# Attention and Fourier-mix kernel: q, k and v loads in half tiles on a new timetable, converted weights stored slot by slot

## The chip, the cores and the metric

The kernel runs on one core of a Trainium2 chip. The metric is the device time of one execution in microseconds (us), lower is better. All times are of undisturbed ("fast") runs.

## The reference, cut to what matters

```python
# q, k, v: (8, 12, 448, 64); x is the attention output as (8, 448, 768)
scores = einsum('bhij,hg->bgij', q @ k^T / 8, w_pre)     # heads mixed before the softmax
attn   = softmax(scores); attn = einsum('bhij,hg->bgij', attn, w_post)   # and after
x      = attn @ v
u      = x + real(fft(fft(x, axis=seq), axis=d_model))
out    = u + relu(layernorm(u) @ w_ch1) @ w_ch2          # w_ch1, w_ch2 arrive as float64
```

## The kernel before

There are two stages. The **mixing stage** does attention and the Fourier mix; the **feed-forward stage** the two large products. The mixing stage is one software pipeline of 192 steps, 24 per batch. In every step TensorE (PE) does a pre-mix product (tile mx), a post-mix product (po), and one or two of QK^T, attention times v (AV) and transposes; VectorE (DVE) a row maximum and a block transpose; ScalarE (ACT) the exponentials and most copies. GpSimd (POOL) has three jobs in one in-order queue: it scales the softmax, it "folds" the rows for the Fourier transform (additions of half and quarter rows), and it issues the DMAs for q, k, v and the weights.

The fold of a batch is dealt from a list. What the step may take of it depends on whether the step also took something from the list of loads:

```python
    while s < TOT or any(fill.values()):
        n = take("none", s)               # loads due in this step (POOL issues them)
        ...                               # premix, postmix, max, exp, AV, transpose
        if s >= 4:
            wts.deal(1)                   # one DVE operation of the weight conversion
        ...                               # QK, gather of step s+4 (SP), scale of step s+2 (POOL)
        for _ in range(min(len(folds), 1 if n and s > 3 else 2)):
            folds.pop(0)()                # one POOL operation (some are three)
        take("full", s)                   # transposes, emit_x, emit_z, emit_s2
        s += 1

    def emit_z(b, par, y):                # Fourier product; needs the whole fold
        while ("xf", par) not in batches[b] or folds:
            folds.pop(0)()
        ...
```

q and k loads are timed from their use, v loads come whole, one pair of heads a step, and a converted weight item (seven tiles) is stored in one DMA:

```python
            old = loads[-4] + 2 if len(loads) > 3 else -99
            for y in range(2):
                due("none", max(old, f + a - GS - 5) + y, lambda ...: emit_load_qk(b, xx, nm, y))
        ...
        for pr in range(3):
            due("none", f + AT_AV[-1][pr] + 2, lambda ...: emit_load_v(b, pr))   # both halves
    ...
        def store():                      # _Weights.add
            nc.gpsimd.dma_start(out=dst.rearrange("k p f -> p k f"), in_=box["st"][:, :, :w])
```

"Local step" means the step within the batch, 0 to 23. The second half of a batch's fold (12 entries) is queued at the end of local step 5 of the *next* batch, and emit_z wants it at the end of local step 14.

## Time and profile before

| | before |
|---|---|
| time, median (range) | 2551.49 us (2550.93 to 2552.16) |
| span of the profiled run | 2549.6 us |
| first block transpose of the pipeline | 43.2 us |
| its 192 steps, first start to last | 900.0 us |
| from the last step's start to the end | 1606.5 us |

The last three rows come from the starts of the DVE block transposes, one per step, in the timeline. Differences between those starts are "step lengths"; a step length holds both a stall and the slow matmuls after it.

The rows of the groups by line for POOL (out<-in, count, busy us and mean ns, then idle before) price what the change moves:

```profile
L569 POOL TENSOR_TENSOR xs<-X 113x384 f32<-113x384 f32 x64 | 64.3, 1019 | 0.3
L374 POOL DMA_DIRECT2D rawk<-in_k_dram x84 | 61.1, 729 | 0.0
L382 POOL DMA_DIRECT2D vv<-in_v_dram x48 | 30.6, 640 | 0.0
L253 POOL DMA_DIRECT2D w<-wst x30 | 28.8, 961 | 117.8 <-DVE wst L250 115.6 <-DVE rcp L475 2.2
```

The reader is to see that issuing a DMA occupies POOL for 0.64 to 0.96 us, about as long as a fold operation (1.02 us). Of q and k 24 DMAs are issued per batch, 17.5 us of POOL time. The 0.0 us of idle time before the k and v issues means that POOL always came to them straight from other work; of these issues only the stores waited.

### The profile page before, as it was taken

The numbers are of one execution on the slowest core, as the hardware profiler recorded it, in microseconds if no ns is written. First come the engines' busy times: TensorE is split into PE (matmuls) and PEld (weight loads), VectorE is DVE, ScalarE is ACT, GpSimd is POOL, SyncE is SP. The second block draws the span as 40 slices with busy tenths as digits, with TensorE's granted clock in tenths as the row PEclk, the third lists the DMA queues.
The fourth block names the chain that finished last, engine by engine and source line by source line (L and its number), as shares of the span: only waits on it lengthen the run. The fifth ranks groups of instructions, "written<-read, shape, count | busy, mean of one in ns | idle before, by whom it ended". The sixth has DMA issues, their size and how long they took to land.

```text
span 2549.6 us, 47913 instructions
## 1 busy us (share of the span) xinstructions
PE 2404.3 (94%) x18608; PEld 1557.3 (61%) x18608; DVE 1513.6 (59%) x3103; ACT 791.8 (31%) x2059; POOL 695.8 (27%) x1112
## 2 busy tenths in 40 slices
PE   6899998979898985999999999999999999999999
PEld 2344443534444444677777777777777777777776
DVE  3666767757677764778456636663666366633333
ACT  3575656646565642232211111111111111011110
POOL 2565758575756652111000000000000000000000
PEclk9899999989899997999999999999999999999999
DMA  4544546363544545544444444444444444343331
GB/s 123 165 152 143 169 134 182 119 170 134 167 153 131 168 140 184 183 152 165 180 145 136 147 155 143 138 147 150 141 146 140 154 136 150 129 155 115 133 112 50
DMA packets 165311, 372.05 MB, mean 146 GB/s; under 512 B 33854, under 2 KB 87126, under 8 KB 165086
## 3 DMA queue, kind: packets, MB, share of 16 engines
q1 hardware_dynamic: 129038, 260.22, 31.0%
q0 software_dynamic: 30480, 107.39, 14.0%
q8 instruction: 149, 2.44, 0.4%
q10 hardware_dynamic: 5568, 1.38, 0.3%
q14 instruction: 76, 0.62, 0.1%
HBM read 211.98 MB, written 74.34 MB: 112 GB/s over the span
## 4 chain that ended last, share of the span: by engine, by line
PE 82%; POOL 5%; ACT 4%; DVE 4%; DMA 3%; issue 2%; SPq 1%; ACTq 0%; POOLq 0%; DVEq 0%
PE psP L896 17%; PE psP L950 17%; PE psR L896 9%; PE psR L950 9%; PE mx L451 6%; PE ms L515 5%; PE psQ L950 4%; PE psQ L896 4%; PE po L488 4%; PE ms L425 3%; ACT PP L467 3%; DMA Kr<-Sb 3%; DVE nmx L459 2%; PE ms L613 1%; PE ms L629 1%
## 5 line engine op out<-in xcount | busy, mean ns | idle before, releaser
L896 PE MATMUL psP<-ub,w1t 128*128 128x256 f32 x2016 | 462.9, 379 | 0.0
L950 PE MATMUL psP<-w2t,h 128*128 128x384 f32 x1344 | 460.9, 486 | 0.0
L896 PEld LDWEIGHTS psP<-ub,w1t 128*128 128x128 f32 x2016 | 382.8, 190 | 60.7
L950 PEld LDWEIGHTS psP<-w2t,h 128*128 128x128 f32 x1344 | 254.4, 190 | 165.9
L478 POOL TENSOR_SCALAR PP<-PP,rcp 128x448 f32<-128x448 f32 x384 | 242.4, 642 | 355.9 <-DVE rcp L476 280.9
L204 POOL DMA_DIRECT2D raw<-in_moe_w_ch_dram x120 | 69.8, 582 | 988.4 <-DVE tmp L242 969.3
L467 ACT ACTIVATE PP<-mx,nmx 128x448 f32<-128x448 f32 x384 | 240.3, 631 | 290.1 <-DVE nmx L459 277.9
L459 DVE TENSOR_REDUCE nmx<-mx 128x1 f32<-128x448 f32 x384 | 221.6, 619 | 148.0 <-PE mx L451 137.7
L956 DVE TENSOR_TENSOR u<-u,psP 128x384 f32<-128x384 f32 x336 | 183.6, 553 | 143.5 <-PE psP L950 141.3
L901 ACT COPY h<-psP 128x512 f32<-128x512 f32 x42 | 24.6, 587 | 761.7 <-PE psP L896 761.7
L451 PE MATMUL mx<-Kr,kw 60*64 60x448 f32 x1536 | 211.4, 566 | 51.8 <-ACT PP L467 39.8
L896 PE MATMUL psR<-ub,w1t 128*128 128x256 f32 x1008 | 231.4, 379 | 0.0
L950 PE MATMUL psR<-w2t,h 128*128 128x384 f32 x672 | 230.5, 486 | 0.0
L499 DVE STREAM_TRANSPOSE Pv<-po 128x896 f32<-128x896 f32 x192 | 212.7, 1108 | 6.7 <-PE po L488 6.7
L896 PEld LDWEIGHTS psR<-ub,w1t 128*128 128x128 f32 x1008 | 191.4, 190 | 26.3 <-DVE ub L875 0.3
L907 DVE TENSOR_TENSOR h<-h,psQ 128x512 f32<-128x512 f32 x42 | 28.9, 688 | 295.5 <-PE psQ L896 295.5
L307 ACT COPY Sb<-ms 124x448 f32<-124x448 f32 x384 | 184.9, 541 | 21.7 <-DMA Kr<-Sb 16.0
L488 PE MATMUL po<-PP,kw 60*32 60x448 f32 x3072 | 191.0, 554 | 0.0
L515 PEld LDWEIGHTS ms<-Pv,vv 64*64 64x64 f32 x5376 | 145.3, 134 | 73.5 <-issue 33.8
L425 PE MATMUL ms<-kT,qT 64*60 64x448 f32 (+1 forms) x1536 | 189.7, 556 | 0.0
L950 PEld LDWEIGHTS psR<-w2t,h 128*128 128x128 f32 x672 | 127.2, 190 | 87.4
L515 PE MATMUL ms<-Pv,vv 64*64 64x120 f32 x5376 | 169.3, 270 | 2.2 <-issue 2.2
(92 smaller groups left out, 2680.8 us busy)
## 6 DMA issues: line engine op xcount, KB each, us to landing
ub<-ub SPq DMA_DIRECT2D x294, 384.0 KB
Kr<-Sb SPq DMA_DIRECT2D x768, 105.0 KB
raw<-in_moe_w_ch_dram POOLq DMA_DIRECT2D x72, 256.0 KB, 3.1
raw<-in_moe_w_ch_dram POOLq DMA_DIRECT2D x48, 384.0 KB, 3.4
w<-wst POOLq DMA_DIRECT2D x18, 896.0 KB, 4.7
w<-wst POOLq DMA_DIRECT2D x12, 1344.0 KB, 5.8
w1t<-w SPq DMA_DIRECT2D x42, 384.0 KB
w2t<-w SPq DMA_DIRECT2D x42, 384.0 KB
```

Source lines behind the costliest of these rows:

```text
L307: (nc.scalar.copy if eng == "a" else nc.vector.tensor_copy)(out=out, in_=in_)
L425: nc.tensor.matmul(pss[x][64 * y:64 * y + r0 + 64 - lo, :S], st["qT", xx][64 * x:64 * x + 64, y, lo:r0 + 64], st["kT", xx][64 * x:64 * x + ...
L451: nc.tensor.matmul(mx[64 * z:64 * z + 64, x, :S], kw1[64 * x:64 * x + KR, :], Kr[64 * x:64 * x + KR, z, :], start=True, stop=True)
L459: nc.vector.tensor_reduce(nmx[:, x:x + 1], steps[T]["mx"][:, x, :S], axis=AX.X, op=ALU.max, negate=True)
L467: nc.scalar.activation(PP[:, x, :], steps[T]["mx"][:, x, :S], ACTF.Exp, bias=steps[T]["nmx"][:, x:x + 1], accum_out=den[:, x:x + 1])
L478: nc.gpsimd.tensor_scalar(PP[:, x, :], PP[:, x, :], rcp[:, x:x + 1], 1.0, op0=ALU.mult, op1=ALU.mult)
L488: nc.tensor.matmul(po[o:o + 32, z, :S], kw2[64 * z:64 * z + KR, y, :], PP[64 * z:64 * z + KR, :, c * HS:(c + 1) * HS], start=True, stop=True)
L499: nc.vector.transpose(g["Pv"][:, T % GT, :].rearrange("p (z s) -> p z s", z=2), steps[T]["po"][:, :, :S])
L515: nc.tensor.matmul(pss[y][64 * x:64 * x + 64, :nu * R], st["v", pr][64 * y:64 * y + 64, x, jb * D:(jb + 1) * D], _ap(Pv, 64 * y * rp + 32 ...
L896: nc.tensor.matmul(p[:, m, :], w1[i][:, kc, m * P:(m + 1) * P], ub[:, kc, :], start=i in OPENS and m == kc == 0, stop=kc == NK - 1, skip_g ...
L950: nc.tensor.matmul(p, lhs[i][:, kf, x * P:(x + 1) * P], w2[i][:, kf, :], start=i in OPENS and kf == 0, stop=kf == FM - 1, skip_group_check ...
L956: nc.vector.tensor_tensor(us_, us_, p, op=ALU.add)
```

## The change

The intent: at most one half tile is loaded a step (only the last two halves of v share one, step 7), and of the steps 6 to 12, in which POOL is to fold the second half, only 8 and 12 have a q or k load; only q and k loads now hold the folding to one operation; a weight item leaves in seven small stores, each a step after the DVE operation that made it.

```diff
+AT_L = ((-4, -3), (-2, -1), (0, 1), (2, 8), (12, 13), (14, 15))   # local steps of the q/k halves
+AT_V = ((3, 4), (5, 6), (7, 7))                                   # and of the v halves
@@ _Weights.add: a tile for each slot, and a store for each slot
+        def new(slot):
+            box[slot] = self.pst.tile([P, DH], F32, name="wst", tag=f"wst{slot}")[:, :w]
+        def store(slot):
+            self.later.append(lambda: nc.gpsimd.dma_start(out=dst[slot], in_=box[slot]))
...
-        self.ops.append((store, False))
@@ deal
+        while self.later:
+            self.later.pop(0)()
         while self.ops and (n > 0 or not self.ops[0][1]):
@@ q/k
-                due("none", max(old, f + a - GS - 5) + y,
+                due("none", f + at[y] - GS,
@@ v
-            due("none", f + AT_AV[-1][pr] + 2, lambda b=b, pr=pr: emit_load_v(b, pr))
+            for y in range(2):
+                due("none", f + AT_V[pr][y], lambda b=b, pr=pr, y=y: emit_load_v(b, pr, y))
@@ take: only q/k loads return True and count
-        n0 = len(fill[kind])
+        large = 0
...
-                fn()
+                large += bool(fn())
...
-        return n0 - len(fill[kind])
+        return large
```

## The prediction

> **What bounds the kernel now.** I read the page first, then stage windows, then the waits, then the timeline around the longest gaps. The slices of the page part the run in two: a talking-heads stage up to about 1000 us, and a feed-forward stage after it.
>
> ```profile
> PE   6899998979898985999999999999999999999999
> POOL 2565758575756652111000000000000000000000
> DMA  4544546363544545544444444444444444343331
> ```
>
> The windows by stage (columns: stretch, length, busy us and count of PE, PEld, DVE, ACT, POOL, granted clock, DMA share, GB/s) say how much either stage has to give:
>
> ```profile
> 480.00:620.00 140.00, 123.72 (x1900) 61.77 (x1896) 99.28 (x191) 82.65 (x250) 91.16 (x140) 0.94 0.49 148
> 1200.00:1800.00 600.00, 599.44 (x2341) 442.40 (x2340) 330.69 (x699) 78.00 (x129) 35.77 (x56) 1.00 0.46 151
> ```
>
> In the second stage PE is busy 599.44 of 600 us. Whatever the change does to weight stores there lies beside PE, so I give that stage 0 us. All the gain must come from the first stage, where PE idles some 12% and its granted clock dips.
>
> The waits, longest in total, name what PE stands still for there:
>
> ```profile
> PE ms L613 <- POOL xf L590: 41.3, 14, 10.2
> PE mx L451 <- ACT PP L467: 39.8, 48, 10.4
> PE ms L548 <- ACT Sb L307: 9.7, 5, 6.5
> PE mx L451 <- DMA Kr<-Sb: 9.7, 11, 3.6
> ```
>
> To see where these lie I took the starts of the 192 DVE transposes (L499) from the timeline: one per step, 24 steps per batch. A clean step takes 3.8 to 4.1 us. Local step 14 takes 13.4, 13.4, 14.1, 13.0, 12.4 and 13.0 us in batches 1 to 6, but 4.5 in batch 7. Three single steps stand out too: batch 0 step 4 (14.4), batch 4 step 5 (13.4), batch 5 step 13 (10.6). Step 14 of batch 6 in the timeline:
>
> ```profile
> 791.74 1.46 POOL L374 DMA_DIRECT2D rawq<-in_q_dram  x2
> 793.24 1.25 POOL L478 TENSOR_SCALAR PP<-PP,rcp 128x448 f32<-128x448 f32 x2
> 796.03 1.46 POOL L374 DMA_DIRECT2D rawk<-in_k_dram  x2
> 797.53 1.25 POOL L478 TENSOR_SCALAR PP<-PP,rcp 128x448 f32<-128x448 f32 x2
> 798.76 3.84 POOL L590 TENSOR_TENSOR xf<-xq 113x385 f32<-113x385 f32 x4
> 799.80 0.69 PE L613 MATMUL ms<-ts,xf 113*97 113x113 f32 x2 [5.24 <-POOL xf L590]
> ```
>
> The reader is to see a POOL queue without a hole: each step it issues q/k loads (0.73 us each), scales (1.25), and does a fold operation; the last four come in one lump and PE waits 5.24 us. The windows of the two steps 13 and 14 without loads (batch 7) and of step 14 with them (batch 6):
>
> ```profile
> 794.00:807.00 13.00, 7.50 (x71) 5.05 (x67) 4.25 (x9) 4.13 (x9) 10.06 (x16) 0.74 0.35 110
> 901.40:909.90 8.50, 8.50 (x145) 4.36 (x141) 5.02 (x11) 5.90 (x18) 2.52 (x4) 1.00 0.34 128
> ```
>
> The same folding, but without loads, leaves PE full and its clock at 1.00. The batch-4 stall is another thing: three pairs of v loads, a store of converted weights and a raw load stand ahead of the gathers (Kr<-Sb).
>
> ```profile
> 506.08 0.99 POOL L253 DMA_DIRECT2D w<-wst  x1 [1.00 <-DVE wst L250]
> 508.32 1.28 POOL L382 DMA_DIRECT2D vv<-in_v_dram  x2
> 511.92 1.25 POOL L382 DMA_DIRECT2D vv<-in_v_dram  x2
> 520.63 0.97 ACT L307 COPY Sb<-ms 124x448 f32<-124x448 f32 x2 [6.79 <-DMA Kr<-Sb]
> 521.22 0.98 PE L548 MATMUL ms<-ident,XT 128*113 128x128 f32 x3 [6.49 <-ACT Sb L307]
> ```
>
> **What the Trainium skill says.** (1) "DMA: Bandwidth & Descriptors", section "Issuing engines are not separate DMA queues": transfers issued from any engine share the same 16 DMA engines and interleave. The trace agrees: POOL's 896 KB store at 506 us is followed by late gathers of SP and the 6.79 us wait. (2) Same page, "Rules for kernel authors": two transfers to disjoint partition halves serialize, so splitting gives no bandwidth. The v halves were two DMAs already (48 of 224 KB), so I credit the halves with timing only. (3) "TensorE: Matmul & The Clock Gate", section "What's actually happening": after about 3.4 us idle the clock gate falls to half and takes as long to open. The trace agrees: after the 6.49 us gap eight mx matmuls take 1.77 us against 0.98, and the window of step 14 shows 0.74. So a stall costs more than its gap, and I price by step lengths, which contain both.
>
> **The change part by part.**
>
> *Folding.* The second half of a batch's fold is 12 entries, queued at local step 5 of the next batch, wanted at the end of step 14. Before, any item of the "none" list in a step cuts the folds from two to one, and q/k loads sit on every step from 5 to 15. So steps 6 to 14 do 9 entries and the rest are popped in a lump: the trace's L590 x4 is one for step 14 and three left over. After, only q/k loads cut the folds. They sit at 20 to 23, 0, 1, 2, 8, 12 to 15. Steps 6 and 7 do two each, 8 one, 9 to 11 two each, 12 one: 12 entries, done two steps early. POOL's work over steps 6 to 12, by the rows (scale 1.26, q/k issue 1.46, v issue 0.64, pairs 1.02, sides 1.0, quarters 1.5, both 0.99, scatter 1.04): 3.9, 5.0, 4.8, 3.3, 3.8, 3.3, 3.9, which is 28.0 us; one raw load and one or two slot stores at about 0.6 make it 29. The same seven steps take 28.4 us in batch 7, where nothing stalls (4.1, 5.0, 3.8, 4.3, 3.6, 3.8, 3.8). So POOL is just full, with step 13 (2.7 us of POOL work) and most of 14 as reserve. I expect no wait of L613. What is left of steps 13 and 14 then: 8.5 us as in batch 7, plus the 1.0 us of the next batch's seven transposes (0.98), which batch 7 has not: 9.5. Now they take 19.0, 18.5, 18.3, 18.4, 23.0 and 17.2, mean 19.1. Saving (19.1 - 9.5) x 6 = 57.6 us, batch 5's stall at 676 us included.
>
> *Weight stores.* Five items in this stage, each one store of 896 or 1344 KB, become 35 of 128 or 192 KB, a deal behind. POOL no longer waits for the last DVE operation (1.00 us at 506), but issues six more DMAs per item at about 0.6 us: 30 x 0.6 = 18 us of POOL time over 160 steps, 0.1 us a step, beside PE. The lump in the DMA queues goes. With v loads at 224 KB a step instead of 448, I expect batch 4 step 5 to fall from 13.4 to 6, like its neighbours: 7.4 us.
>
> *Start.* Batch 0 step 4 loses 10.5 us while DVE waits 11.76 us for a raw weight load behind v, tables and v. Ahead of it now stand 448 + 785 + 448 KB plus 512 of its own; after, 224 + 785 + 224 + 512, a fifth less: 2 us. Against it, q/k loads of batch 1 now start in the prologue, as soon as raw buffers come free, beside batch 0's last q and k loads, for which PE waits 3.59 us: minus 1.5 us, a guess.
>
> *Rest.* Step 12 of batches 1 to 6 averages 4.65 us against 3.8 in batch 7; I take a third of that: 2 us. For new collisions (v halves now land two steps before use, 8 to 9 us, against 5.1 us to land) I take off 4.
>
> Sum: 57.6 + 7.4 + 2 - 1.5 + 2 - 4 = 63.5; I round down for the thin POOL margin to 60.5: 2551.5 - 60.5 = 2491.0 us.
>
> **The rivals.** *A: POOL is still the bound.* The work is moved, not removed: 29 us of work stand against 28.4, so L613 could still wait 2 or 3 us a batch, with a colder clock. For it: L569 rises from 1.02 to as much as 1.32 us when DVE runs beside it. Against: the reserve of step 13. It would make 2505 to 2515. *B: v becomes the wait.* Its halves come at steps 3 to 7 for use at 6, 8, 9; with POOL behind by a step, AV (L515) would wait 1 to 3 us in each of 7 batches: 2500 to 2510. *C: the stalls were DMA volume, not POOL.* Then early loads collide with gathers elsewhere (steps 20 to 2) and the step table shows new long steps: 2510 to 2530. Against it: in batch 6 step 14 the DMA share is only 0.35. *D: better*, the start stall vanishes too: 2480.
>
> **Range and chances.** A and B overlap with half the sum's uncertainty, about 12 us each way; a gain under 25 us needs C. The 2% line is 2551.5 x 0.98 = 2500.5, 9.5 us above my figure. So 2491, range 2474 to 2512; faster by 2% 0.77, within 2% 0.22, slower 0.01.
>
> **What would show it.** Right: no wait of L613 on xf over 1 us in batches 1 to 6, step 14 near 5.5 us, granted clock near 1.0 there; no 6 us wait of ACT on Kr<-Sb near 515 us; second stage still 599 of 600. Wrong: L613 still waiting (A), L515 or its weight loads waiting for vv (B), steps 20 to 2 over 5 us with Kr<-Sb as releaser (C), or a longer prologue than the 43 us to the first L499.

## The result, and the profile after

| | before | after |
|---|---|---|
| time, median (range), 4 runs each | 2551.21 us (2550.54 to 2552.16) | 2482.79 us (2478.94 to 2491.94) |
| ratio, 95% interval | | 0.9737 (0.9708 to 0.9766) |
| span of the profiled run | 2549.6 us | 2483.8 us |
| first block transpose | 43.2 us | 45.7 us |
| 192 steps | 900.0 us | 831.2 us |
| rest | 1606.5 us | 1606.9 us |

A ratio is the mean time of one kernel's fast runs over that of the other's of the same rounds, so not quite the ratio of the medians quoted. The change is faster by 2.6%, and all of it is in the 192 steps; the prologue is 2.5 us longer.

Of the page after, two of the same slices; then, of its windows, a stretch of the mixing stage, one of the feed-forward stage, and steps 13 and 14 of batch 6 (columns: length, busy us of PE, PEld, DVE, ACT, POOL, clock, DMA share, GB/s):

```profile
PE   6899999999999949999999999999999999999999
POOL 3477867768675541121011001100110011000000
```

```profile
480.00:620.00 140.00, 132.67 (x2021) 63.75 (x2021) 116.67 (x220) 90.59 (x274) 107.22 (x170) 1.00 0.57 173
1150.00:1700.00 550.00, 549.44 (x2142) 404.51 (x2141) 303.75 (x641) 71.42 (x118) 62.38 (x113) 1.00 0.47 149
733.60:743.70 10.10, 9.42 (x114) 4.12 (x110) 6.80 (x15) 6.74 (x19) 7.78 (x15) 1.00 0.58 177
```

The clock column is the granted TensorE clock, 1.00 being full speed. In the first stretch PE now works 132.67 of 140 us instead of 123.72, with the clock at 1.00 instead of 0.94. Steps 13 and 14 take 10.1 us, with PE busy for 9.42, though there is more DMA traffic in them (177 GB/s) than in the 13.0 us of the old step 14 alone (110). The feed-forward stage is as full as before.

Of the waits of PE, longest in total (who waited for whom, us, times, longest):

```profile
PE mx L462 <- ACT PP L478: 42.2, 51, 9.8
PE psQ L878 <- ACT un L869: 21.4, 1, 21.4
PE ms L624 <- POOL xf L601: 10.6, 2, 10.3
PE mx L462 <- DMA Kr<-Sb: 4.6, 6, 1.6
```

The Fourier product (L613 before, L624 now) waited 41.3 us for the fold; of the 10.6 us that remain, 10.3 are one wait at 898 us, after the last step, which the kernel before had too (10.2 us). In the timeline, step 14 of batch 6:

```profile
737.24 1.45 POOL L385 DMA_DIRECT2D rawk<-in_k_dram  x2
739.00 1.80 PE L624 MATMUL ms<-ts,xf 113*97 113x113 f32 x16
740.55 1.25 POOL L489 TENSOR_SCALAR PP<-PP,rcp 128x448 f32<-128x448 f32 x2 [1.86 <-DVE rcp L487]
```

No wait stands behind the 16 Fourier matmuls, and POOL, not PE, is the one that idles (1.86 us).

Where the time went, in step lengths (batches 1 to 6, then 7, which has no q/k loads; us, from the timelines):

```
local step   before                               after                                before b7   after b7
5            3.8  6.2  6.2 13.4  5.1  6.1         3.8  5.2  5.1  5.1  5.2  5.1           5.8         5.1
10           3.8  4.1  3.5  3.7  3.8  3.6         4.7  4.0  3.8  4.7  5.6  4.5           3.6         3.8
13           5.6  5.1  4.2  5.4 10.6  4.2         3.8  4.8  3.8  3.8  3.8  4.8           4.1         4.0
14          13.4 13.4 14.1 13.0 12.4 13.0         5.2  5.9  5.2  5.3  6.8  5.3           4.5         4.4
```

Summed over all batches: step 14 gains 45.4 us, step 5 12.1, step 13 10.3, step 6 5.2, steps 20 to 22 another 5.2; step 10 loses 5.0 and step 0 2.8. A second trace of the changed kernel (a2_change_again, below) tells what of this repeats: steps 14, 5, 13 and 6 gain 46.9, 12.1, 11.6 and 5.4 us there, and step 10 loses 4.2; but step 0 loses only 0.2, and steps 20 to 22 lose 2.0 instead of gaining. The sums of a few us at steps 0 and 20 to 22 are scatter between traces.

### The profile page after: what moved, and what is told of

It reads as the page before. It is cut to its first block, busy times and chain, and to the rows that moved or that the text cites.

```text
span 2483.8 us, 48361 instructions
## 1 busy us (share of the span) xinstructions
PE 2378.0 (96%) x18608; PEld 1538.6 (62%) x18608; DVE 1519.1 (61%) x3103; ACT 787.2 (32%) x2059; POOL 778.7 (31%) x1292
## 4 chain that ended last, share of the span: by engine, by line
PE 82%; DVE 5%; ACT 4%; DMA 4%; POOL 3%; issue 1%; SPq 1%; ACTq 0%; POOLq 0%; DVEq 0%
PE psP L907 18%; PE psP L961 17%; PE psR L907 9%; PE psR L961 9%; PE mx L462 6%; PE psQ L961 4%; PE psQ L907 4%; PE ms L526 4%; PE po L499 4%; ACT PP L478 3%; PE ms L436 3%; DVE nmx L470 3%; DMA Kr<-Sb 2%; PE ms L640 2%; PE ms L624 1%
## 5 line engine op out<-in xcount | busy, mean ns | idle before, releaser
L462 PE MATMUL mx<-Kr,kw 60*64 60x448 f32 x1536 | 205.2, 560 | 49.5 <-ACT PP L478 42.2
L526 PEld LDWEIGHTS ms<-Pv,vv 64*64 64x64 f32 x5376 | 142.2, 132 | 68.9 <-issue 30.7
L526 PE MATMUL ms<-Pv,vv 64*64 64x120 f32 x5376 | 164.3, 267 | 0.0
```

Source lines behind the costliest of these rows:

```text
L462: nc.tensor.matmul(mx[64 * z:64 * z + 64, x, :S], kw1[64 * x:64 * x + KR, :], Kr[64 * x:64 * x + KR, z, :], start=True, stop=True)
L526: nc.tensor.matmul(pss[y][64 * x:64 * x + 64, :nu * R], st["v", pr][64 * y:64 * y + 64, x, jb * D:(jb + 1) * D], _ap(Pv, 64 * y * rp + 32 ...
```

## The experiments

Twelve more runs were made, eleven of other kernels and one of the changed kernel again, all with correct results. Each is given by its ratio to the kernel before in its own rounds; the changed kernel stands at 0.9737, and at 0.9731 (0.9709 to 0.9753) when it was run again beside the last three.

### Each part alone, and each part undone

**e3_loads_alone**: the kernel before with the new q/k times and nothing else.

```diff
-                due("none", max(old, f + a - GS - 5) + y,
+                due("none", f + at[y] - GS,
```

> The kernel before with only the new times of the q/k loads; v whole, stores in one burst, gate as before. Theory (POOL queue full of q/k issues while it folds): the L613 waits of batches 1 to 6 go, steps 13 and 14 together fall from 19 to about 10 us, some 50 us in all, so about 2500 us; the stall at batch 4 step 5 (13.4 us) stays because v and the store burst are untouched. Rival (DMA volume of v and stores makes the stalls): under 15 us of gain, 2537 or more.

Measured: 2497.16 us, ratio 0.9804 (0.9778 to 0.9830). Step 14 falls to 5.2 to 5.5 us in batches 1 to 6, and the trace gains 53.5 us in all. The stall of batch 4 stays (step 5: 12.0 us); of the waits of PE:

```profile
PE ms L549 <- ACT Sb L308: 6.9, 4, 5.1
```

So the q/k times carry three quarters of the gain by the ratios, four fifths by the traces, as the theory said; the batch-4 stall is another matter, of v and stores. This kernel still counts v loads too when it holds the folding to one; no run undoes that new counting alone, but step 14 evidently does not need it.

**e2_stores_alone**: the kernel before with only the slot-by-slot stores (the `_Weights` part of the diff).

> The kernel before with only the slot-by-slot stores. Theory: the long step of batch 4 (13.4 us) falls to about 7 and step 13 of batch 5 (10.6) to about 5, but the six L613 waits stay or grow a little, as POOL issues 30 more stores of 0.6 us: 2540 us, give or take 5. Rival (the stores cause the main loss): 2510 or less.

Measured: 2548.02 us, ratio 1.0012 (0.9986 to 1.0037): no gain in the timed runs, 7 us in the one trace. The trace shows the two expected reductions (batch 4 step 5 from 13.4 to 6.4, batch 5 step 13 from 10.6 to 5.9), and step 14 giving 6.1 us back: PE's waits for the fold grow from 41.3 to 47.0 us. That the 30 more issues in a POOL queue that was late already do this is my reading; no run isolates it. The rival that the stores made the main loss is out. The gain of 11 us I expected did not come.

**u3_stores_undone**, **u2_v_undone**, **u1_loads_undone**: the changed kernel with one part put back.

```diff
 u3: the _Weights class of the kernel before
 u2: -AT_V = ((3, 4), (5, 6), (7, 7))
     +AT_V = ((3, 3), (4, 4), (5, 5))
 u1: -                due("none", f + at[y] - GS,
     +                due("none", max(old, f + a - GS - 5) + y,
```

> The changed kernel with only the stores put back into one burst per item. Theory: a burst of 896 or 1344 KB now meets v halves instead of whole v, so a stall returns once or twice: 3 to 10 us slower than the changed kernel, 2486 to 2494 us. Rival (bursts never mattered once loads moved): within 2 us of the changed kernel, or faster by the saved POOL issues and by fewer waits of DVE at local step 10.

> The changed kernel with v loaded whole at local steps 3, 4 and 5 again (both halves in one step). Theory: steps 5 and 6 go back from 5.1 and 3.9 to about 6 and 4.1 us in batches 2 to 6, because gathers wait behind 448 KB instead of 224 KB: 4 to 8 us slower than the changed kernel, about 2489. Rival (v timing does nothing once the stores are small): within 2 us.

> The changed kernel with only the q/k loads put back to their old steps (5 to 15). Theory: step 14 goes back to 13 us or more in batches 1 to 6 and the prologue is 2.5 us shorter again: 40 to 55 us slower than the changed kernel, 2523 to 2538. Rival (v and stores made the gain): under 20 us slower.

| kernel | median us | ratio (95%) | batch 4 step 5 |
|---|---|---|---|
| u3, bursts back | 2484.61 | 0.9751 (0.9733 to 0.9769) | 5.1 |
| u2, v whole again | 2489.91 | 0.9751 (0.9732 to 0.9770) | 5.2 |
| u1, old q/k times | 2535.63 | 0.9935 (0.9918 to 0.9952) | 5.1 |
| e3, both back, and the old counting | 2497.16 | 0.9804 (0.9778 to 0.9830) | 12.0 |
| changed kernel | 2482.79 | 0.9737 (0.9708 to 0.9766) | 5.1 |

u1 loses nearly all, as expected: step 14 is back at 11.6 to 15.4 us. u3 is a miss of mine and a win for its rival: the stores by slot are worth nothing that can be measured here once v comes in halves. u2's ratio lies within the intervals too; its trace is 10.7 us longer than the changed kernel's, but spread over single steps (batch 7 step 5: 8.2 us against 5.1) rather than in the steps 5 and 6 of batches 2 to 6 that I had named. The column of batch 4 step 5 settles most of the double part: with whole v *and* the burst the gathers (SP's loads of Kr) come too late; with the burst alone gone (e2: 6.4 us beside 13.4) or with the burst back but v in halves (u3) they do not. The two measures insure against the same stall. One reserve: e3 and u3 differ in the counting of loads too, so what the halves do is not isolated as cleanly as what the stores do.

### What made PE wait at step 14: the rule, or POOL's time?

**e1_gate_off_before**: the kernel before with the rule of one fold a step taken off; no load moves.

```diff
-            for _ in range(min(len(folds), 1 if n and s > 3 else 2)):
+            for _ in range(min(len(folds), 2)):
```

> The kernel before with the gate on folding taken off: always up to two fold operations a step, loads unmoved. Rival gate theory (POOL had room, only the rule of one fold a step left a lump of four): the L613 waits go, 45 us gained, about 2505 us. Own theory (POOL itself is full in these steps: 27.9 of 30.4 us busy before the lump): only the 2.4 us idle per batch can be used, at most 15 us gained, 2536 to 2556 us, and the delayed scales and loads may cost as much.

Measured: 2518.13 us, ratio 0.9875 (0.9852 to 0.9897): 32 us gained, between the two theories and twice what mine allowed. Of the waits of PE:

```profile
PE ms L613 <- POOL xf L590: 10.4, 2, 10.1
PE ms L548 <- POOL XT L537: 7.7, 5, 2.4
```

The first line: no fold wait is left but the late one, and step 14 is 5.2 to 8.1 us; it gains 43.6 us summed. The second is new: the X transposes now wait for a small POOL memset, and steps 10 to 12 lose 23.4 us. The fold was in time, and the rest of POOL's queue (scales, memsets) became late in its place: in steps 10 to 12 of batches 1 to 6 POOL was busy for 93.0 of 94.9 us (72.7 of 73.3 in the kernel before, which had fewer folds to do there). And since no load moved while step 14 lost its stall, the DMA traffic of the loads did not by itself make it.

**d2_gate_one**: the changed kernel with one fold in every step, so that a lump is left for step 14 although the loads are away.

```diff
-            for _ in range(min(len(folds), 1 if n and s > 3 else 2)):
+            for _ in range(min(len(folds), 1 if s > 3 else 2)):
```

> The changed kernel with one fold operation a step always, so that three of the twelve are left for step 14. POOL has time, only the order changes. Theory: L613 waits about 2 to 3 us a batch for the lump of three or four (0.99 us each): 15 to 25 us slower, 2498 to 2508. Rival (the gate does not matter once the loads are away): under 5 us slower; and the DVE waits at local step 10 may go, which gives 3 us back.

Measured: 2526.95 us, ratio 0.9903 (0.9878 to 0.9927), the trace 44.5 us longer, twice what I expected. One line of the waits of PE, then two of batch 7 in the timeline, then the window of this step 14:

```profile
PE ms L624 <- POOL xf L601: 40.8, 16, 10.3
```

```profile
882.17 0.69 PE L624 MATMUL ms<-ts,xf 113*97 113x113 f32 x2 [3.86 <-POOL xf L601]
883.12 2.94 PE L624 MATMUL ms<-ts,xf 112*97 112x112 f32 x14 [0.26 <-POOL xf L601]
```

```profile
877.72:889.08 11.36, 7.24 (x56) 3.78 (x52) 2.60 (x7) 3.26 (x8) 5.68 (x8) 0.70 0.20 76
```

The fold waits are back. Batch 7 has no q/k loads at all, yet its step 14 goes from 4.4 to 11.4 us: the wait of 3.86 us, and then 14 matmuls in 2.94 us where 16 took 1.80. This is the clock gate that the Trainium skill describes ("TensorE: Matmul & The Clock Gate", section "What's actually happening": about 3.4 us of idleness close it); the trace agrees: the clock of this step is 0.70, where it is 1.00 in the changed kernel. Of the 6.9 us that the step loses, 4.1 are waits, and the slower clock is left for most of the rest; over seven batches step 14 loses 46.2 us, 6.6 a batch. So **the lump alone, with POOL otherwise idle for 1.6 us a step in batch 7, makes almost the whole stall**: step 14 takes 11.6 to 12.9 us in batches 1 to 6, against 12.4 to 14.1 before.

**d1_pool_time**: the changed kernel with POOL time added, and no DMA, in steps 6 to 14.

```diff
+            if s >= GS and 6 <= s % GS <= 14:
+                for _ in range(7):
+                    nc.gpsimd.memset(pad[:, :], 0.0)          # pad: [128, 120]
             for _ in range(min(len(folds), 1 if n and s > 3 else 2)):
```

> The changed kernel with seven small memsets on POOL (about 1.4 us together) in each of local steps 6 to 14 of batches 1 to 7: the POOL time of the q/k issues comes back without their DMA traffic. Theory (POOL time is what made PE wait): 12.6 us more POOL work per batch against about 6 us of reserve, so L613 waits on xf come back at 4 to 7 us a batch in batches 1 to 6 with a cold clock behind them: 25 to 50 us slower, 2508 to 2533. Rival (it was the DMA traffic of the loads): no L613 wait over 1 us, under 5 us slower.

Measured: 2545.80 us, ratio 0.9976 (0.9959 to 0.9992), the trace 61.8 us longer, of which 8.8 lie after the last step, where the memsets run on by the way the condition is written. The groups by line and the waits of PE:

```profile
L768 POOL MEMSET pad<- 128x120 f32 x518 | 102.8, 198 | 25.7
PE po L500 <- POOL PP L490: 23.8, 22, 3.4
PE ms L560 <- POOL XT L549: 21.6, 7, 3.4
```

102.8 us of memsets are 1.4 us a step, the price of two q/k issues. They cost 52 us within the steps and move no byte, so POOL's time alone is enough to cost that much. By itself this does not clear the DMA traffic of the loads; e1, where the loads stayed and the stall at step 14 went, does that for step 14. But the expected form of the loss did not come: with two folds a step the fold was in time, and PE waited for scales (po) and for the memset of XT, at steps 9, 11 and 13.

Together: POOL's in-order queue had no room left in steps 10 to 12, and the rule of one fold a step decided *where* PE paid for it. As the lump at step 14 it was the dearest place.

### A better version

Three things in the trace after were left: the longer prologue, the stall of batch 0 step 4 (12.9 us; 10.2 in a2's trace, with 2.0 more at step 3), and step 10. **f3_start** moves batch 1's q/k halves to steps -1 to 11 and the tables of the Fourier transform from step 3 to 17; **f4_start_fold** also holds local step 10 to one fold; **f5_start_fold_burst** is f4 with the single-burst stores of the kernel before.

```diff
 f3: +            if b == 1:
     +                at = {10: (-1, 0), 12: (1, 2), 14: (8, 9), 16: (10, 11)}.get(a, at)
     -    due("none", 3, emit_tables)
     +    due("none", 17, emit_tables)
 f4: -... 1 if n and s > 3 else 2)):
     +... 1 if s > 3 and (n or s % GS == 10) else 2)):
 f5: f4 with the _Weights class of the kernel before
```

> The changed kernel unaltered, for a fair base beside the next three: 0.974 of the kernel before, 2479 to 2490 us.

> The changed kernel with two edits for the start: batch 1's q/k loads at steps -1 to 11 instead of -4 to 8, and the tables at step 17 instead of 3. Theory (the longer prologue comes from POOL's early loads beside batch 0's last q load; the stall at batch 0 step 4 from the tables ahead of the first raw weights): first L510 start back from 45.7 to about 43.2 us, batch 0 step 4 from 12.9 to 5 or 6 us, together 8 to 10 us faster than the changed kernel, about 2475. Rival (the stall is the first raw load's own 512 KB and v, not the tables): step 4 stays over 9 us, gain under 4 us.

> As f3_start, and one fold operation instead of two in local step 10, so that the last of the twelve is done at step 13. Theory (two folds in a row keep DVE's weight operation waiting at step 10): the 0.2 to 1.8 us excess of step 10 goes in batches 1 to 6, 2 to 5 us faster than f3_start, if step 13's fold does not make L613 wait. Rival: step 14 waits again for the fold, 3 us or more slower than f3_start.

> As f4_start_fold, with the stores back in one burst per item. From the earlier run with only the stores undone (0.9751 against 0.9737, the trace 1 us shorter) I expect no difference beyond 3 us from f4_start_fold; a rival in which bursts matter makes it 5 us or more slower.

| kernel | median us (range) | ratio (95%) |
|---|---|---|
| a2_change_again | 2484.61 (2478.34 to 2487.33) | 0.9731 (0.9709 to 0.9753) |
| f3_start | 2481.43 (2475.29 to 2483.47) | 0.9715 (0.9694 to 0.9737) |
| f4_start_fold | 2478.93 (2472.31 to 2482.55) | 0.9713 (0.9690 to 0.9737) |
| f5_start_fold_burst | 2476.29 (2470.29 to 2478.99) | 0.9699 (0.9678 to 0.9720) |

f3's mechanism holds and its size does not: step 4 of batch 0 falls from 12.9 to 6.4 us and the prologue from 45.7 to 44.4, but 2.2 us come back at step 18, just after the tables, and the trace gains 4.4 us (3.4 against that of a2), not 8 to 10. From the three timelines of the prologue, the transposes of batch 0's last q tile, in the kernel before, the changed kernel and f3 (the wait in brackets):

```profile
17.92 1.73 PE L402 MATMUL ms<-ident,rawq 128*128 128x128 f32 x7 [3.59 <-DMA rawq<-in_q_dram]
```

```profile
20.79 1.73 PE L413 MATMUL ms<-ident,rawq 128*128 128x128 f32 x7 [6.61 <-DMA rawq<-in_q_dram]
```

```profile
18.07 1.73 PE L413 MATMUL ms<-ident,rawq 128*128 128x128 f32 x7 [3.69 <-DMA rawq<-in_q_dram]
```

The early loads of batch 1 delay the last load of batch 0, and moving them undoes it (so does u1, with the old q/k times: 3.24 us). f4's fold rule is inconclusive: step 10 itself does not move (0.2 us against f3), steps 11 and 12 gain 3.3 us, step 13 loses 1.2. If this is an effect, it comes a step or two later than I had placed it; between two traces of one kernel single sums move as much. f5 is the fastest kernel; against the changed kernel's 0.9731 the intervals still overlap, so that only the direction is read from it: 8 us by the medians, 6.4 us in the traces. Against f4, from which it differs in the stores alone, it is 2.6 us by the medians, within the 3 us expected. That it does without the slot stores agrees with u3.

## Why the prediction was right

The time, 2482.79 us, lies in the range, 8 us below the point, and "faster by over 2%" was the likeliest of the three. By its steps:

- **The feed-forward stage gives nothing: right.** 549.44 of 550 us busy, and the rest of the run 0.4 us longer.
- **Folding, 57.6 us: right in size.** Steps 13 and 14 together average 9.75 us in batches 1 to 6 (9.0, 10.7, 9.0, 9.1, 10.6, 10.1) against the 9.5 predicted, so (19.07 - 9.75) x 6 = 55.9 us. Reading the floor from batch 7, which does the same folding without the loads, was what made this close (9.3 in the second trace). Batch 5's stall at step 13 is booked in it; this one falls from 10.6 to 5.6 us by the loads alone (e3) and to 5.9 by the stores alone (e2), so it was not the folding's alone.
- **Its mechanism: half right.** The prediction named both the lump and a POOL without room, "just full" even after the change. It put POOL's work of steps 6 to 12 at 29 us against 28.4; in the changed kernel POOL is busy for 26.4 of 30.0 us there (mean of batches 1 to 6), so near full, but with some room. And e1 shows that the lump was the larger part: with the rule off the same work gains 32 us. POOL's time was the rest, paid at steps 10 to 12 in e1 (23.4 us) and, in the change, only 6.1 us there.
- **Weight stores, 7.4 us at batch 4 step 5: right there (8.3), but credited to both parts together.** u3 keeps the 5.1 us with the burst restored, e2 gets most of it with v whole: one of the two suffices.
- **Start: 2 us expected at step 4, 1.5 measured (2.2 with steps 3 and 4 together in the second trace); the prologue 2.5 us longer (3.1) against 1.5 guessed.** The predicted collision is the 6.61 us wait shown above. A longer prologue stood among the signs of being wrong, although the sum itself had priced one: that sign came, and did not decide anything.
- **Rest and collisions: the mis-sized terms.** Step 12 did not gain the 2 us (it lost 0.4). The 4 us set aside for collisions were spent at step 10 (5.0; 4.2 in the second trace). Steps 5 and 6 gained 9.0 us besides batch 4's stall (12.1 + 5.2 - 8.3), of which the sum had nothing, and the 3 us taken off for POOL's margin were not needed. These 12 us, less what step 12, the start and the folding fell short and small amounts elsewhere, leave the gain of the traces (65.8) 5 us above the predicted 60.5; by the medians it is 8. That the point came so near is in part luck: misses of both signs cancelled.
- **Rivals:** A did not happen (no fold wait within the steps), B did not (no wait of L526 for vv among PE's waits), C hardly (step 0, 1.3 us at most in one batch, and not in the second trace), and D's end of the start stall came only when f3 moved the tables.

## What to carry to other kernels

POOL computed and issued its DMAs here from one in-order queue, and an issue cost it as much as a small operation (0.64 to 0.96 us against 1.02); on such an engine, look at what stands ahead of the work that the critical engine will wait for, and move the issues, which have slack, away from it. A rule that spreads work over steps must end with nothing left over: the remainder falls due in one lump at the consumer, and a wait near 4 us can be paid almost twice, since the matmuls behind it run slow (d2, batch 7: 4.1 us of waits, a step 6.9 us longer). When two parts of a change cure the same stall, undo each by itself before crediting either.

## What the Trainium skill lacked or had wrong

- "DMA: Bandwidth & Descriptors", section "Issuing engines are not separate DMA queues", calls the sequencer time to initiate a DMA usually small relative to the DMA. As a comparison that holds here (q and k: 0.73 us of issue, 3.5 to 3.9 us from issue to landing). What the section does not say is that this time comes out of the work of an engine that also computes: 24 q/k DMAs a batch at 0.73 us, and d1, which gave 1.4 us a step back to POOL without any DMA, lost 52 us.
- Same page: no figure tells the issue time by shape. Measured on POOL: 0.56 us (a slot of 128 rows; 0.60 in the mixing stage), 0.64 (v half), 0.73 (q or k, rows of 256 bytes), 0.96 (seven slots at once).
- Same page, "Rules for kernel authors", on two transfers to disjoint halves: no gain in bandwidth. No run here tests that, since v goes out as two half DMAs in every kernel. What the rule does not weigh is when the halves are issued: in separate steps instead of one, with the burst in place, batch 4 step 5 took 5.1 us (u3) instead of 12.0 (e3, which differs in the counting of loads too).
- "SBUF — State Buffer", section "SBUF: two separate sides", has DVE operations with two SBUF inputs and GpSimd operations that read SBUF exclude each other. The traces fit an exclusion, but no run isolates it: with two folds back to back, the 384-wide additions of the weight conversion rose from 518 to 818 ns in the mean (eight each, in the windows 100 to 900 and 100 to 840 us). The section gives the ports to the operation that starts first; the starts in the profile do not tell it so simply. One of these additions in the timeline after starts before two folds and is itself the one that stretches, to 1.82 us (another, at 608.74 us, took 0.52, and the fold that began 0.06 us behind it 1.32):

```profile
612.84 1.82 DVE L261 TENSOR_TENSOR wst<-wst 128x384 f32<-128x384 f32 x1
613.22 1.02 POOL L580 TENSOR_TENSOR xs<-X 113x384 f32<-113x384 f32 x1
614.32 1.21 POOL L585 TENSOR_TENSOR xs<-xs 113x383 f32<-113x383 f32 x1
```
